# Attention over two problems on one core: a new start, new load costs and a new projection rate

## Chip, cores, metric

One core of a Trainium2 chip. The metric is the device time of one launch in microseconds (us). The four executions of one kernel lie within 0.6 to 7.7 us of each other. The experiments ran on several chips; each is given as a ratio to the kernel before, run beside it on the same chip.

## The reference, cut to what matters

Two problems, A and B, of the same shapes, each a cross-attention against a stored K and V:

```python
# B=16 batches, Sq=144 queries, D=448, H=16 heads, Sk=512 keys, Dh=256, bf16
q = (x @ wq).reshape(B, Sq, H, Dh).transpose(0, 2, 1, 3)
scores = jnp.einsum("bhqd,bhkd->bhqk", q, k_cache) * (Dh ** -0.5)
p = softmax(scores)
o = jnp.einsum("bhqk,bhkd->bhqd", p, v_cache)
out = o.transpose(0, 2, 1, 3).reshape(B, Sq, H * Dh) @ wo
# result: concatenate([A's out, B's out], axis=-1)
```

K and V are 16 x 16 x 512 x 256 values each per problem: 268 MB in all, read once.

## The kernel before

A *unit* is one (problem, batch, head). Units 0 to 255 are A, 256 to 511 are B. For each unit TensorE computes Q (a head of x times wq), S = K Q, P.V, row sums, and some units later a few pieces of the output projection. Exponentials are ScalarE's, most evictions VectorE's.

Every load goes through one queue in program order, issued by SyncE. If the load at its head has to wait for a buffer, all behind it wait too. There are these loads:

- K of the first 48 units in its natural form (2 units a load, 512 KB), transposed by TensorE. They use the same ring of 9 buffers as V.
- From unit 48 on, K by transposing loads of 16 units (4.2 MB), called *K waves* here: wave 0 for unit 48, wave 13 for unit 256 (B's first), wave 15 for unit 288.
- V, 2 units a load, 512 KB. x in groups of batches, wq by heads, wo in 8 parts. B's wq and wo can be loaded only when A's are used up.

The order in the queue is made when the kernel is built, by a planner that gives each load an estimated duration:

```python
def t_load_v(G):
    sl = v_seq["v", G] % NV                  # NV = 9 buffers, shared with natural K
    ...
    S.add(SP, e, writes=[(("v", sl), ("v", G))], dma_sem="v%d" % sl, name="v%d" % G)
...
load(first_q[g0], ..., 1.3 + 0.55 * (g1 - g0), t_load_x, XG)
load(u0 - ls(u0), ..., 2.0 + 0.97 * (u1 - u0), t_load_k, W)
load(first_h[pr, h0], ..., 0.65 * (h1 - h0), t_load_wq, pr, h0, h1)
load(wo_use[pr, wg], ..., 1.3, t_load_wo, pr, wg)
load(UV * G, None, 1.44, t_load_v, G)
```

The projection's pieces are spread over the units by a rate; a piece is done when there is credit:

```python
OP_DELAY, OP_START, OP_RATE = 2, (28, 16), (1.04, 1.15)
...
credit += OP_RATE[i >= NU + OP_START[1]] * NCH * NWO / NU
```

## Time and profile before

| | before |
|---|---|
| time, median of the three executions known then (range) | 1055.7 us (1053.1 to 1056.2) |
| TensorE busy | 1029.9 us, 98% of the span |
| matmuls at their pitch | 1024.3 us |
| lost before the last matmul | 21.8 us |
| of it ahead of unit 16, at unit 288 | 10.9 us, 9.2 us |
| load engines busy | nine tenths or more in every slice but the last two |

The useful quantity is *lost time*: the start of a matmul in the trace, less what all matmuls before it take at their pitch (their usual time from start to start). The 34 constant matmuls and the 24 transposes of x of the new kernel are not counted as work here. Lost time stays flat where TensorE is fed, and each hole is a step in it. The pitches are rounded: with the medians of the trace (0.0625, 0.1225, 0.189 and 0.056 us) the sum is 1020.6 us and the loss 25.5, the difference being spread evenly over the span. So its steps, and differences between kernels at one unit, say more than its absolute value. A wait is given below either as the idle time that a view shows or as the time between two matmul starts over the pitch, which is some 0.2 us more. The two busy rows together say that two resources are busy nearly all the time, TensorE and the loads.

### The profile page before, as it was taken

How to read it: one execution, taken by the hardware profiler on the slowest of the kernel's cores; microseconds unless marked ns; L12 is line 12 of the kernel's file. 1: busy time of each engine (PE TensorE's matmuls, PEld its weight loads, DVE VectorE, ACT ScalarE, POOL GpSimd, SP SyncE). 2: the span in 40 equal slices, each digit the busy share in tenths (PEclk: the TensorE clock that was granted, in tenths of full speed). 3: DMA queues.
4: the chain of work that ended last, by engine and by line, in shares of the span. 5: the costliest groups of instructions: out<-in, count | busy, mean ns of one | idle time of the engine just before them, and what ended most of it. 6: DMA issues, size and time to landing. Idle time of an engine off the chain costs nothing.

```text
span 1051.6 us, 32329 instructions
## 1 busy us (share of the span) xinstructions
PE 1029.9 (98%) x12376; PEld 875.8 (83%) x12376; DVE 737.7 (70%) x2039; ACT 794.1 (76%) x2365; POOL 636.2 (61%) x1030
## 2 busy tenths in 40 slices
PE   7999999999999999999999799999999999999998
PEld 6999888888888888888888688888888888888885
DVE  5776676777776776676777567677776667777775
ACT  5877677777777787777877567787877777788785
POOL 3555556666666666666756456566666666666673
PEclk9999999999999999999999999999999999999999
DMA  9999999999999999999999999999999999999950
GB/s 291 363 341 340 263 306 266 288 288 293 290 300 284 285 237 257 302 290 297 265 288 340 268 276 300 295 272 300 282 269 269 299 258 305 302 271 257 289 187 14
DMA packets 591748, 294.14 MB, mean 280 GB/s; under 512 B 502592, under 2 KB 516768, under 8 KB 591584
## 3 DMA queue, kind: packets, MB, share of 16 engines
q1 hardware_dynamic: 591584, 291.99, 110.1%
q8 instruction: 99, 1.62, 0.6%
q14 instruction: 65, 0.53, 0.2%
HBM read 161.48 MB, written 4.13 MB: 157 GB/s over the span
## 4 chain that ended last, share of the span: by engine, by line
PE 90%; DMA 6%; SPq 1%; ACT 1%; DVE 1%; issue 0%; POOL 0%; ACTq 0%; DVEq 0%
PE s_ps L1112 23%; PE ot_ps L1168 23%; PE qp_ps L1081 22%; PE op_ps L1284 19%; DMA kt_sb<-in_B_k_cache_dram 2%; DMA kt_sb<-in_A_k_cache_dram 2%; PE ot_ps L1184 2%; DMA wq_sb<-in_A_wq_dram 1%; PE qp_ps L1032 1%; PE s_ps L1032 1%; PE qp_ps L1284 1%; ACT rinv_sb L1205 1%; DMA v_sb<-in_B_v_cache_dram 0%; SPq L1002 0%; ACT pt_sb L1122 0%
## 5 line engine op out<-in xcount | busy, mean ns | idle before, releaser
L1132 POOL TENSOR_TENSOR pp_sb<-pt_sb 128x288 f32<-128x288 bf16 x512 | 384.6, 751 | 320.1 <-ACT pt_sb L1122 305.4
L1122 ACT ACTIVATE pt_sb<-s_ps 128x288 bf16<-128x288 f32 x1024 | 364.6, 408 | 182.7 <-PE s_ps L1112 176.5
L1220 DVE TENSOR_TENSOR ring<-ot_ps,rinv_sb 128x288 bf16<-128x288 f32 (+2 forms) x640 | 241.8, 394 | 159.4 <-ACT rinv_sb L1205 155.0
L1112 PE MATMUL s_ps<-qt_sb,kt_sb 128*128 128x144 bf16 x4096 | 341.3, 227 | 8.0 <-DMA kt_sb<-in_B_k_cache_dram 6.9
L1168 PE MATMUL ot_ps<-pt_sb,v_sb 128*128 128x144 bf16 x4096 | 340.2, 226 | 0.3 <-DMA v_sb<-in_A_v_cache_dram 0.2
L1112 PEld LDWEIGHTS s_ps<-qt_sb,kt_sb 128*128 128x128 bf16 x4096 | 288.3, 98 | 60.0 <-issue 7.3
L1205 ACT ACTIVATE rinv_sb<-ln_sb 64x144 f32<-64x144 f32 x928 | 298.3, 321 | 24.2
L1081 PE MATMUL qp_ps<-xt_sb,wq_sb 128*128 128x288 bf16 (+1 forms) x2368 | 302.3, 271 | 2.2 <-DMA wq_sb<-in_A_wq_dram 1.2
L1284 PE MATMUL op_ps<-wo_sb,ring 128*128 128x448 bf16 x1120 | 285.5, 352 | 0.0
L1081 PEld LDWEIGHTS qp_ps<-xt_sb,wq_sb 128*128 128x128 bf16 x2368 | 212.7, 98 | 77.1 <-DVE qt_sb L1094 2.3
L1168 PEld LDWEIGHTS ot_ps<-pt_sb,v_sb 128*128 128x128 bf16 x4096 | 274.3, 98 | 1.2 <-DMA v_sb<-in_A_v_cache_dram 0.4
L1137 POOL TENSOR_TENSOR p_sb<-pp_sb 128x144 f32<-128x144 f32 x464 | 227.4, 490 | 74.2 <-DVE ps_sb L1146 9.4
L1235 DVE TENSOR_REDUCE run_sb<-ot_ps 128x1 bf16<-128x144 f32 x560 | 146.5, 304 | 76.7 <-ACT ln_sb L1192 42.6
L1146 DVE TENSOR_TENSOR ps_sb<-p_sb 64x144 bf16<-64x144 f32 x464 | 156.1, 336 | 45.8 <-POOL p_sb L1137 32.5
L1095 DVE CAST qt_sb<-qp_ps 128x576 bf16<-128x576 f32 x216 | 162.1, 750 | 14.0 <-PE qp_ps L1081 10.9
L1284 PEld LDWEIGHTS op_ps<-wo_sb,ring 128*128 128x128 bf16 x1120 | 93.7, 98 | 20.1
L1192 ACT ACTIVATE ln_sb<-ot_ps 128x144 f32<-128x144 f32 x232 | 67.9, 293 | 32.3 <-PE ot_ps L1184 24.5
L1184 PE MATMUL ot_ps<-ps_sb,ones 128*128 128x144 bf16 x280 | 63.3, 226 | 0.0
L1094 DVE CAST qt_sb<-qp_ps 128x288 bf16<-128x288 f32 x80 | 35.8, 447 | 2.8 <-PE qp_ps L1081 2.6
L1040 ACT ACTIVATE kt_sb<-qp_ps 128x512 bf16<-128x512 bf16 x48 | 28.9, 603 | 6.1 <-PE qp_ps L1032 6.1
L1137 POOL TENSOR_TENSOR ps_sb<-pp_sb 128x144 bf16<-128x144 f32 x48 | 23.5, 490 | 6.9 <-PE ot_ps L1184 0.3
L1184 PEld LDWEIGHTS ot_ps<-ps_sb,ones 128*128 128x128 bf16 x280 | 27.4, 98 | 0.0
(29 smaller groups left out, 154.5 us busy)
## 6 DMA issues: line engine op xcount, KB each, us to landing
v_sb<-in_A_v_cache_dram SPq DMA_DIRECT2D x128, 512.0 KB, 6.9
v_sb<-in_B_v_cache_dram SPq DMA_DIRECT2D x128, 512.0 KB, 7.0
v_sb<-in_A_k_cache_dram SPq DMA_DIRECT2D x22, 512.0 KB, 9.9
out_dram<-ost_sb SPq DMA_DIRECT2D x36, 112.0 KB, 6.1
wo_sb<-in_A_wo_dram SPq DMA_DIRECT2D x8, 448.0 KB, 8.5
wo_sb<-in_B_wo_dram SPq DMA_DIRECT2D x8, 448.0 KB, 8.7
wq_sb<-in_B_wq_dram SPq DMA_DIRECT2D x4, 768.0 KB, 9.3
wq_sb<-in_A_wq_dram SPq DMA_DIRECT2D x3, 768.0 KB, 9.2
```

Of the source, the lines that this page charges most:

```text
L1081: ins = t.matmul(acc, lhsT=wq_sb[:, kc, c0:c0 + 128], rhs=xt_sb[:, kc, xo:xe + 1:max(xe - xo, 1), :], start=(kc == 0), stop=(kc == 3))
L1095: return v.tensor_copy(qt_sb[:, a:b + 1:b - a, :, :], qp_ps[:, :, 0:2 * SQ].rearrange("p e (u q) -> p u e q", u=2))
L1112: ins = t.matmul(s_ps[bank][:, (c % 2) * SQ:(c % 2 + 1) * SQ], lhsT=kt_sb[:, 2 * c + dc, ko:ko + 128], rhs=qt_sb[:, qsl, dc, :], start=(dc ...
L1122: return a.activation(pt_sb[:, psl, 2 * k:2 * k + 2, :].rearrange("p b q -> p (b q)"), s_ps[bank][:, 0:2 * SQ], AF.Exp, scale=DH ** -0.5)
L1132: return g.tensor_tensor(pp_sb[:, :, :], pt_sb[:, psl, 0:2, :], pt_sb[:, psl, 2:4, :], op=ALU.add)
L1137: return g.tensor_tensor(dst, pp_sb[:, 0, :], pp_sb[:, 1, :], op=ALU.add)
L1146: return v.tensor_tensor(ps_sb[p0:p0 + 64, sl, :], p2_sb[0:64, :], p2_sb[64:128, :], op=ALU.add)
L1168: ins = t.matmul(ot_ps[ob][:, dc * SQ:(dc + 1) * SQ], lhsT=v_sb[:, vsl, j, c * DH + dc * 128:c * DH + (dc + 1) * 128], rhs=pt_sb[:, sl, c, ...
L1205: return a.activation(rinv_sb[p0:p0 + 64, sl, :], ln_sb[h0:h0 + 64, :], AF.Exp, scale=-1.0)
L1220: ins = v.tensor_tensor(ring[:, 2 * h:2 * h + 2, r0:r0 + q1 - q0], ot_ps[ob][:, 0:2 * SQ].rearrange("p (c q) -> p c q", c=2)[:, :, q0:q1], ...
L1235: return v.tensor_reduce(run_sb[:, k, j:j + 1], ot_ps[ob][:, 2 * SQ:3 * SQ], axis=AX.X, op=op)
L1284: ins = t.matmul(acc[0:m, 0:D], lhsT=ring[:, c, col0:col0 + m], rhs=wo_sb[:, c, :], start=(c == op_first), stop=(c == op_last))
```

## The change

Five parts. Intent of each: (A) get TensorE to its first P.V sooner: the first two batches of x come by a plain load and are transposed on TensorE, constant matmuls bring the clock up, ScalarE issues the first wq loads. (B) better load costs in the planner, and a rule that puts a load of x right behind a K wave; this also places one more V load ahead of wave 0. (C) fewer projection pieces in units 200 to 240, more in 240 to 292, so that TensorE needs the waves around the problem boundary later. (D) the second Q of a step moves behind P.V. (E) the last eviction is shared by VectorE and ScalarE.

Cut to its core, with three comments added:

```diff
-    OP_DELAY, OP_START, OP_RATE = 2, (28, 16), (1.04, 1.15)
-    MARGIN, HOLD = 1.0, 1.0
+    WARM = 34
+    XR, X_AT = 48, {0: -4, 1: -3}
+    OP_DELAY, OP_START, OP_RATE = 2, (28, 16), ((200, 1.04), (240, 0.7), (292, 1.5), (600, 1.1))
+    MARGIN, HOLD, K_FIX = 1.0, 1.0, 2.4
 ...
+            t_load_wq(0, 0, 1, ACT)
+            t_load_wq(0, 1, 2, ACT)
 ...
+                for _ in range(WARM):
+                    ins = t.matmul(op_ps[:, 0:128], lhsT=ones[:, :], rhs=ones[:, :], start=True, stop=True)
 ...
+        def t_load_xn(g):          # plain load of x, 48 rows to a partition block
+        def t_tr_x(g):             # 12 transposes on TensorE, evicted by VectorE then ScalarE
 ...
-                load(first_q[g0], ..., 1.3 + 0.55 * (g1 - g0), t_load_x, XG)
+                load(first_q[g0], ..., 2.0 + 0.55 * (g1 - g0), t_load_x, XG)
-                load(u0 - ls(u0), ..., 2.0 + 0.97 * (u1 - u0), t_load_k, W)
+                load(u0 - ls(u0), ..., K_FIX + 0.97 * (u1 - u0), t_load_k, W)
-                    load(first_h[pr, h0], ..., 0.65 * (h1 - h0), t_load_wq, pr, h0, h1)
+                    load(first_h[pr, h0], ..., 0.78 * (h1 - h0), t_load_wq, pr, h0, h1)
 ...
-        first = [(t_load_n, (0, 0)), (t_load_x, (0,)), (t_load_wq, (0, 0, 1)), (t_load_n, (0, 1))]
+        first = [(t_load_xn, (0,)), (t_load_n, (0, 0)), (t_load_n, (0, 1)), (t_load_xn, (1,))]
 ...
+                if after_k and m[3] is t_load_x and start <= now:
+                    best = (start, latest, m, lo)
+                    break
 ...
-            now += m[2] - (1.0 if m[3] is t_load_k and dma_plan and dma_plan[-1][0] is t_load_k else 0.0)
+            now += m[2] - (1.4 if after_k and m[3] in (t_load_k, t_load_x) else 0.0)
 ...
-            for u in of_step(lq, i):
+            for u in of_step(lq, i)[:1]:
 ...
+            for v in of_step(lq, i)[1:]:      # behind P.V
+                if q_pair(v):
+                    t_q(v)
+                    t_evac_q(v)
```

More of the change, by code (lines that the diff above doesn't have):

```diff
@@ L798, in bass_concat_heads__mha_block_cached__gqa_block_cached__near_ridge_kernel @@
     assert KR % KW == 0 and NU % KW == 0 and KW % KG == 0
-    X_GROUPS = ((0, 1), (1, 2), (2, 6), (6, 10), (10, 14), (14, 18), (18, 20), (20, 24), (24, 28), (28, 32))
+    X_GROUPS = ((2, 6), (6, 10), (10, 14), (14, 18), (18, 20), (20, 24), (24, 28), (28, 32))
     assert X_GROUPS[-1][1] == NP * Bn and H == KW
-    WQ_GROUPS = ((0, 1), (1, 2), (2, 4), (4, 8), (8, 12), (12, 16))
+    WQ_GROUPS = ((2, 4), (4, 8), (8, 12), (12, 16))
+    WARM = 34
     NQT, NPT, NPS, NRI, NOST = 11, 4, 2, 2, 2
@@ L868, in bass_concat_heads__mha_block_cached__gqa_block_cached__near_ridge_kernel @@
             sem_names.append("n%d" % i)
+        for i in range(NX):
+            sem_names.append("xn%d" % i)
         for i in range(NWG):
@@ L911, in t_init, with e3 @@
             S.add(DVE, e2, writes=[("wqz", 0)], name="wqz")
+            def e3(g):
+                return g.memset(xt_sb[64:128, 3, :, :], 0.0)
+            S.add(DVE, e3, writes=[(("xt", g), g) for g in range(NX)], name="xz")
             def e4(g):
@@ L915, in t_init, with e6 @@
             S.add(POOL, e4, writes=[("ones", 0)], name="ones")
+            def e6(t):
+                ins = None
+                for _ in range(WARM):
+                    ins = t.matmul(op_ps[:, 0:128], lhsT=ones[:, :], rhs=ones[:, :], start=True, stop=True)
+                return ins
+            S.add(PE, e6, reads=[("ones", 0)], writes=[("opp", ("warm", 0))], banks=["op"], name="FAR")
             def e5(g):
@@ L920, in t_init, with t_load_wq @@
             S.add(POOL, e5, reads=[("ones", 0)], writes=[id_key], name="ident")
-        def t_load_wq(pr, h0, h1):
+        def t_load_wq(pr, h0, h1, eng=SP):
             cols = slice(h0 * DH, h1 * DH)
@@ L930, in e @@
                 return q.dma_start(wq_sb[0:64, 3, cols], w[384:448, cols]).then_inc(sems[sem], 16)
-            S.add(SP, e, writes=[(("wq", h), pr) for h in range(h0, h1)], dma_sem=sem, n_dma=2,
+            S.add(eng, e, writes=[(("wq", h), pr) for h in range(h0, h1)], dma_sem=sem, n_dma=2,
                   name="wq%d.%d" % (pr, h0))
@@ L941, in e @@
                     sems["wo%d" % wg], 16)
-            S.add(SP, e, writes=[(("wo", wg), pr)], dma_sem="wo%d" % wg, name="wo%d.%d" % (pr, wg))
+            over = [(("xn", g), 1) for g in range(NX) if pr == 0 and wg in x_rows(g)[2]]
+            S.add(SP, e, writes=[(("wo", wg), pr)] + over, dma_sem="wo%d" % wg, name="wo%d.%d" % (pr, wg))
         def t_load_x(XG):
@@ L977, in t_load_x, with x_rows, e, e1 @@
                   name="x%d" % XG)
+        def x_rows(g):
+            n = SQ // XR
+            c0 = NWO - (NX - g) * n
+            return n, wo_sb[0:XR, c0:c0 + n, :], sorted(set(c // WOG for c in range(c0, c0 + n)))
+        def t_load_xn(g):
+            n, dst, _wgs = x_rows(g)
+            def e(q):
+                return q.dma_start(dst, xs[0][g].rearrange("(t p) d -> p t d", p=XR)).then_inc(sems["xn%d" % g], 16)
+            S.add(SP, e, writes=[(("xn", g), 0)], dma_sem="xn%d" % g, name="xn%d" % g)
+        def t_tr_x(g):
+            n, src, _wgs = x_rows(g)
+            acc = op_ps[:, :].bitcast(BF16)[:, 0:4 * SQ].rearrange("p (c q) -> p c q", c=4)
+            def e(t):
+                ins = None
+                for c in range(4):
+                    m = min(128, D - c * 128)
+                    for k in range(n):
+                        ins = t.transpose(acc[0:m, c, k * XR:(k + 1) * XR], src[:, k, c * 128:c * 128 + m],
+                                          ident[0:XR, 0:XR])
+                return ins
+            S.add(PE, e, reads=[(("xn", g), 0), id_key], writes=[("opp", ("x", g))], banks=["op"], name="TX%d" % g)
+            def e1(v):
+                return v.tensor_copy(xt_sb[:, 0:3, g, :], acc[:, 0:3, :])
+            S.add(DVE, e1, reads=[("opp", ("x", g))], writes=[(("xt", g), g)], banks=["op"], name="exd%d" % g)
+            def e2(a):
+                return a.activation(xt_sb[0:64, 3, g, :], acc[0:64, 3, :], AF.Copy)
+            S.add(ACT, e2, reads=[("opp", ("x", g))], writes=[(("xt", g), g)], banks=["op"], name="exa%d" % g)
         def t_load_k(W):
@@ L1299, in t_evac_op, with e @@
             key = "opp" if bank == "op" else "qp"
-            if eng == ACT:
-                def e(a):
-                    return a.activation(ost_sb[0:m, sl, :], acc[0:m, 0:D], AF.Copy)
-            else:
-                def e(v):
-                    return v.tensor_copy(ost_sb[0:m, sl, :], acc[0:m, 0:D])
-            S.add(eng, e, reads=[(key, ("o", r))], writes=[(("ost", sl), r)], banks=[bank], name="eop%d" % r)
+            parts = ((ACT, 0, D),) if eng == ACT else ((DVE, 0, D // 2), (ACT, D // 2, D))
+            for eng, c0, c1 in parts:
+                def e(g, eng=eng, c0=c0, c1=c1):
+                    if eng == ACT:
+                        return g.activation(ost_sb[0:m, sl, c0:c1], acc[0:m, c0:c1], AF.Copy)
+                    return g.tensor_copy(ost_sb[0:m, sl, c0:c1], acc[0:m, c0:c1])
+                S.add(eng, e, reads=[(key, ("o", r))], writes=[(("ost", sl), r)], banks=[bank], name="eop%d" % r)
         def t_store(r):
@@ L1342, in op_schedule @@
                 fifo["op"].sort(key=lambda t: t[0])
-                credit += OP_RATE[i >= NU + OP_START[1]] * NCH * NWO / NU
+                credit += next(r for u, r in OP_RATE if i < u) * NCH * NWO / NU
                 if i >= NT - H - 14:
@@ L1400, in load_list @@
             for XG, (g0, g1) in enumerate(X_GROUPS):
-                load(first_q[g0], (g1 - NX) * H - lq(NT) if g1 > NX else s_min, 1.3 + 0.55 * (g1 - g0), t_load_x, XG)
+                load(first_q[g0], (g1 - NX) * H - lq(NT) if g1 > NX else s_min, 2.0 + 0.55 * (g1 - g0), t_load_x, XG)
             for W, (u0, u1) in enumerate(WAVES):
                 last = u1 - 1 - KR
-                load(u0 - ls(u0), last - ls(last) + 1 if last >= 0 else s_min, 2.0 + 0.97 * (u1 - u0), t_load_k, W)
+                load(u0 - ls(u0), last - ls(last) + 1 if last >= 0 else s_min, K_FIX + 0.97 * (u1 - u0), t_load_k, W)
             for pr in range(NP):
                 for h0, h1 in WQ_GROUPS if pr == 0 else [(h, h + 4) for h in range(0, H, 4)]:
-                    load(first_h[pr, h0], NU - H + h1 - lq(NU) if pr else s_min, 0.65 * (h1 - h0), t_load_wq, pr, h0, h1)
+                    load(first_h[pr, h0], NU - H + h1 - lq(NU) if pr else s_min, 0.78 * (h1 - h0), t_load_wq, pr, h0, h1)
                 for wg in range(NWG):
                     load(wo_use[pr, wg], wo_done[pr - 1, wg] + 1 if pr else s_min, 1.3, t_load_wo, pr, wg)
+            for g in X_AT:
+                load(X_AT[g], s_min, 0.4, t_load_xn, g)
             for u in range(4):
@@ L1426, in bass_concat_heads__mha_block_cached__gqa_block_cached__near_ridge_kernel @@
             best = None
+            after_k = len(dma_plan) and dma_plan[-1][0] is t_load_k
             for m in todo[:60]:
@@ L1470, in bass_concat_heads__mha_block_cached__gqa_block_cached__near_ridge_kernel @@
                 t_store(stores.pop(0)[0])
+            for g in X_AT:
+                if X_AT[g] == i:
+                    t_tr_x(g)
             u = i + LT
```

## The prediction

> **What bounds the kernel now.** I read the page's first part, then the slices, then the waits, the chain and the timeline around each wait. The first part says that TensorE is busy for nearly the whole span:
>
> ```profile
> PE 1029.9 (98%) x12376; PEld 875.8 (83%) x12376; DVE 737.7 (70%) x2039; ACT 794.1 (76%) x2365; POOL 636.2 (61%) x1030
> ...
> DMA  9999999999999999999999999999999999999950
> ```
>
> Matmul busy time is no proof of a full engine, so I laid the matmul starts in the trace beside the program order. Start to start they are 0.063 us for a 144-column matmul, 0.123 for 288 columns, 0.190 for the output projection and 0.056 for a K transpose. All 12,376 of them at these pitches come to 1024.3 us. The last one starts at 1046.1 us, so 21.8 us are lost before it, and 5.5 us follow it (last eviction and store). Where the 21.8 us lie: 9.2 before unit 0's first P.V matmul, 10.9 by unit 16, 12.1 by unit 48, 12.5 by unit 272, 21.7 by unit 288, and then no more. So there are two holes, the start and one place near 600 us. In the waits view (engine, line waited for: us, times, longest):
>
> ```profile
> PE s_ps L1112 <- DMA kt_sb<-in_B_k_cache_dram: 6.9, 1, 6.9
> ...
> PE s_ps L1032 <- DMA v_sb<-in_A_k_cache_dram: 6.1, 2, 3.9
> ...
> PEld qp_ps L1081 <- DVE qt_sb L1094: 2.3, 7, 1.1
> ...
> PE qp_ps L1081 <- DMA wq_sb<-in_A_wq_dram: 1.2, 2, 0.9
> ...
> PE s_ps L1112 <- DMA kt_sb<-in_A_k_cache_dram: 0.3, 1, 0.3
> ```
>
> The first line is the hole at 600 us; the lines of v_sb and wq_sb are the start; the longest wait for qt_sb, 1.1 us, is one place, at 112 us, where two Q projections in one step wait for one bank. The chain of waits names the two K waves (a wave is the transposing load of K for 16 units) that arrived just too late: start, time to landing.
>
> ```profile
> 96.78 20.41 DMA kt_sb<-in_A_k_cache_dram
> ...
> 576.58 25.29 DMA kt_sb<-in_B_k_cache_dram
> ```
>
> And the timeline shows what the start and the hole look like:
>
> ```profile
> 1.27 1.32 SPq L964 DMA_TRANSPOSE xt_sb<-in_A_x_dram  x1
> ...
> 3.92 0.60 PE L1032 MATMUL s_ps<-qt_sb,v_sb 128*128 128x128 bf16 x4 [3.92 <-DMA v_sb<-in_A_k_cache_dram]
> ...
> 4.50 1.21 SPq L964 DMA_TRANSPOSE xt_sb<-in_A_x_dram  x1
> ...
> 7.49 1.17 PE L1081 MATMUL qp_ps<-xt_sb,wq_sb 128*128 128x144 bf16 x8
> ...
> 13.79 0.66 PE L1081 MATMUL qp_ps<-xt_sb,wq_sb 128*128 128x144 bf16 x8
> ...
> 602.01 1.12 PE L1112 MATMUL s_ps<-qt_sb,kt_sb 128*128 128x144 bf16 x8 [6.88 <-DMA kt_sb<-in_B_k_cache_dram]
> ...
> 603.88 2.12 PE L1081 MATMUL qp_ps<-xt_sb,wq_sb 128*128 128x288 bf16 x8
> ...
> 608.35 0.66 PE L1112 MATMUL s_ps<-qt_sb,kt_sb 128*128 128x144 bf16 x8
> ```
>
> Eight equal matmuls take 1.17 us at 7.49 and 0.66 at 13.79, and after the 6.9 us wait 1.12 us until about 606.5: the array runs at half speed after idling. So the hole costs 7.0 us of wait and 2.2 us of slow matmuls, 9.2 us.
>
> **What the Trainium skill says.** "TensorE: Matmul & The Clock Gate", section "What's actually happening": the array runs at half clock until it has been busy for a window of about 3.4 us, and falls back after an idle one. The trace agrees: 5 us of slow matmuls from 7.1 to 12.4 us, 4.5 us from 602.0. "DMA: Bandwidth & Descriptors", section "Issuing engines are not separate DMA queues": issuing from ScalarE saves only the issuing engine's time. The trace has what can be saved: two x transposes held SyncE 1.32 and 1.21 us, each wq issue 0.57 us. "PSUM — Partial Sum Buffer", section "Terms": two engines on the same bank and partitions at once collide, reads included. So a split eviction has to be serial, and the new program does make ScalarE's half wait for VectorE's.
>
> **The change part by part.** The matmul counts are the same but for 34 constant matmuls and 24 small x transposes, and every matmul that follows has the same pitch.
>
> *Start.* The constants begin at about 1.1 us (their operand is written by 1.0 us) and fill the array to 1.1 + 34 x 0.107 = 4.7 us (0.107 us is the start-to-start time of 128-column matmuls before 12 us), so it is at full speed by about 6. But the first Q is not earlier: x's 12 transposes (about 1 us) start at 4.7, their eviction is VectorE then ScalarE (some 0.45 + 0.3 us plus hand-overs), and the second x's transposes, which stand ahead of the first Q on TensorE, wait for that: the first Q at about 7.5, as now. From there, steps run at full speed (Q 0.5, S 0.5, evictions 0.45 between) instead of half: P.V of unit 0 at about 12.7 against 15.0. The loads also run ahead: the first V lands at 14.4 us now, although 2.8 MB at 0.385 MB/us from 3 us on would be there at 10.3; I take 3.5 us for that lead. The stalls of units 0 to 16 (1.7 us now) are all on loads and should mostly go. Lead at unit 16: about 3.5 us.
>
> *First K wave.* The new order puts one more V load (1.35 us, landing to landing) ahead of it. That load waits for the P.V of unit 37 and is therefore early only as TensorE is. Wave: 117.2 + 1.2 - 3.5 = 114.9 us, or by the backlog of loads 114.6. Needed: 116.8, less 1.07 for the second Q moved behind P.V, less 3.5, is 112.2. So TensorE waits some 2.6 us at unit 48, and of the lead only 117.3 - 114.8 = 2.5 us remain.
>
> *Problem boundary.* Eight wo loads, four wq pairs and 17 V loads lie between two waves here. Landing to landing, now: wave at 517.5, next 559.5, next 601.9, that is 42.0 and 42.3 us. The rate change moves projection pieces in program order: at unit 240 the new kernel has done 28 fewer (x 0.19 = 5.3 us earlier), at unit 272 the same number, at unit 288 some 12 more (2.3 us later). Chain in the new order: wave for unit 240 at 481.1 (now 486.8; gate 5.7 us earlier, its x load moved behind it), unit 256 at 481.1 + 28.5 = 509.6, unit 272 at 509.6 + 42.0 + 2 V (2.7) = 554.3 against a need of 560.6, unit 288 at 554.3 + 42.3 + one store (0.4) = 597.0. Need: 594.9 now without the wait, + 2.3 - 2.5 = 594.7. A wait of 2.3 us remains in place of 7.0, too short, I think, for the half clock. Unit 304's wave: 597.0 + 25.8 + V, store and x load (4.2) = 627.0, need about 629. After that the slack grows. Saved here: 9.2 - 2.3 = 6.9 us.
>
> *End.* The last eviction is one 0.62 us instruction; halved and serial it is two of about 0.35 us and a hand-over: 0.15 us more.
>
> Sum: 2.5 + 6.9 - 0.15 = 9.2 us. From 1055.7 that is 1046.5; as the three runs scatter over 3 us and the profiled one took 1053.4, I say 1046.
>
> **Rivals.** (a) Both waits vanish: the full lead of 3.5, the 1.07 and 0.5 us at unit 48, and 9.2 us: 14 us, 1042 us. For it: all later waves have 6 to 12 us of slack now, and the rates look chosen to fit. Against: the landing sums above. (b) Loads become the bound at the boundary: the faster stretch 200 to 240 needs 16 units in 30 us, and a wave (17.3 us from the landing before it to its own) plus 8 V (10.8), a store and a share of x also take about 30 us. If each load is 1 us worse than I took it, the wait at unit 288 returns to 5 or 6 us with the half clock, and unit 304 waits too: gain 2 to 4 us, 1052. Against: the wave for unit 272 has 6 us of slack even then. (c) The start gives nothing, because the first wave takes all of it back: then only the boundary counts, 1048.5. (d) ScalarE, which now issues four wq loads (about 2.2 us) ahead of its first eviction, delays the opening; it is idle until 4.99 us now, so at most a few tenths.
>
> **Range and chances.** The floor is 1024.3 of matmuls, about 7 at the start with the x transposes, and 5.5 at the end: 1037, plus 2 to 3 between span and time, 1040. Two per cent faster would be 1034.6, under that floor, so it is nearly excluded; slower by 2% would need new waits of 30 us. Range 1040.5 to 1051.5.
>
> **What would show it.** Right: the first Q at 7 to 8 us but its eight matmuls in 0.66; a TensorE wait of 2 to 3 us for the A wave near 112 us; the B wave wait at unit 288 down to 0 to 4 us and no slow matmuls behind it; lost time over pitch about 12.5 us. Wrong: no wait near 112 us (the start's lead was then kept), another wait at unit 272 or 304, or slow matmuls around 600 us.

## The result, and the profile after

| | before | after |
|---|---|---|
| time, median of 4 runs each (range) | 1054.8 (1053.1 to 1056.2) | 1057.3 (1056.4 to 1058.7) |
| ratio, 95% interval | | 1.0026 (1.0005 to 1.0046) |
| span of the profiled run | 1051.6 | 1055.4 |
| lost time at unit 511 | 21.9 | 25.4 |

A ratio is the mean time of one kernel's fast runs over that of the other's fast runs of the same rounds, so it is not quite the ratio of the two medians. Nothing was gained; if anything the kernel is a quarter of a per cent slower. The prediction was 1046.0.

Two lines of the page of the kernel after: busy time of the engines, and the chain of waits by engine.

```profile
PE 1033.3 (98%) x12434; PEld 877.9 (83%) x12434; DVE 738.3 (70%) x2042; ACT 794.4 (75%) x2368; POOL 635.9 (60%) x1030
...
PE 86%; DMA 11%; ACT 1%; SPq 1%; DVE 1%; issue 0%; POOL 0%; ACTq 0%; DVEq 0%
```

TensorE is as full as before, and 11% of the chain is now loads (6% before). Its waits (engine, line, what for: us, times, longest):

```profile
PE ot_ps L1220 <- DMA v_sb<-in_B_v_cache_dram: 5.0, 2, 3.8
PE s_ps L1164 <- DMA kt_sb<-in_A_k_cache_dram: 3.7, 1, 3.7
PE s_ps L1164 <- DMA kt_sb<-in_B_k_cache_dram: 3.2, 3, 2.3
PE op_ps L1018 <- DMA wo_sb<-in_A_x_dram: 2.0, 1, 2.0
```

The wait for B's K fell from 6.9 us to 2.3. Four other waits took its place: for V of B, for A's first K wave, for two more waves of B, and for the plain load of x (it lands in the space of wo). The chain shows when these loads were issued and how long they took (start, us to landing):

```profile
2.21 5.75 DMA wo_sb<-in_A_x_dram
...
95.92 22.49 DMA kt_sb<-in_A_k_cache_dram
...
578.35 25.02 DMA kt_sb<-in_B_k_cache_dram
...
608.87 27.28 DMA kt_sb<-in_B_k_cache_dram
```

And the timeline of TensorE at the places where time was lost (start, us, what; in brackets the idle time just before):

```profile
4.80 0.74 PE L1018 MATMUL op_ps<-qt_sb,wo_sb 48*128 48x48 bf16 x12
...
8.09 0.58 PE L1018 MATMUL op_ps<-qt_sb,wo_sb 48*128 48x48 bf16 x12 [2.00 <-DMA wo_sb<-in_A_x_dram]
...
8.98 1.17 PE L1133 MATMUL qp_ps<-xt_sb,wq_sb 128*128 128x144 bf16 x8
...
15.54 0.66 PE L1220 MATMUL ot_ps<-pt_sb,v_sb 128*128 128x144 bf16 x8
...
118.55 1.12 PE L1164 MATMUL s_ps<-qt_sb,kt_sb 128*128 128x144 bf16 x8 [3.66 <-DMA kt_sb<-in_A_k_cache_dram]
119.46 1.17 PE L1220 MATMUL ot_ps<-pt_sb,v_sb 128*128 128x144 bf16 x8
...
603.50 0.66 PE L1164 MATMUL s_ps<-qt_sb,kt_sb 128*128 128x144 bf16 x8 [2.30 <-DMA kt_sb<-in_B_k_cache_dram]
...
761.51 0.66 PE L1220 MATMUL ot_ps<-pt_sb,v_sb 128*128 128x144 bf16 x8 [3.82 <-DMA v_sb<-in_B_v_cache_dram]
```

The constants did bring the clock up: the transposition of x at 4.80 is followed by fast ones. But the second one waits 2.0 us for its load, and the first Q behind it takes 1.17 us for eight matmuls, half speed again. The first P.V stands at 15.5 us, against 15.0 before. At 118.55 the first K wave is 3.7 us late and the clock is slow for two groups behind it. At 603.5 the wait is short and the clock stays up. At 761.5 there is a wait that the kernel before does not have.

Lost time in us by the start of a unit, in profiled runs (the last two columns belong to experiments told below):

| unit | before | after | after, again | wave 0 moved |
|---|---|---|---|---|
| 40 | 10.6 | 9.1 | 10.5 | 7.6 |
| 64 | 12.0 | 14.4 | 15.9 | 8.3 |
| 200 | 11.8 | 14.2 | 15.7 | 8.1 |
| 280 | 12.5 | 15.9 | 17.3 | 9.7 |
| 288 | 21.7 | 18.3 | 21.4 | 12.0 |
| 511 | 21.9 | 25.4 | 22.2 | 15.6 |

So by unit 64 the change has lost 2.4 us where it should have gained 2.5; at unit 288 it saves most of the big hole as foreseen; and behind it, where the kernel before loses nothing, this run lost 7 us more. In the repeat (third column) it lost 0.8 us there, so that part is chance, as told below.

### The profile page after: what moved, and what is told of

Read it like the earlier page. It is cut to its first block, busy times and chain, and to the rows that moved or that the text cites. A ratio compares the mean times of both kernels' runs of the same rounds, so it can differ in the third digit from the quotient of the medians.

```text
span 1055.4 us, 32451 instructions
## 1 busy us (share of the span) xinstructions
PE 1033.3 (98%) x12434; PEld 877.9 (83%) x12434; DVE 738.3 (70%) x2042; ACT 794.4 (75%) x2368; POOL 635.9 (60%) x1030
## 4 chain that ended last, share of the span: by engine, by line
PE 86%; DMA 11%; ACT 1%; SPq 1%; DVE 1%; issue 0%; POOL 0%; ACTq 0%; DVEq 0%
PE s_ps L1164 22%; PE ot_ps L1220 22%; PE qp_ps L1133 21%; PE op_ps L1336 17%; DMA kt_sb<-in_B_k_cache_dram 8%; DMA kt_sb<-in_A_k_cache_dram 2%; PE ot_ps L1236 1%; PE s_ps L1084 1%; PE qp_ps L1084 1%; DMA v_sb<-in_B_v_cache_dram 1%; PE qp_ps L1336 1%; DMA wo_sb<-in_A_x_dram 1%; ACT rinv_sb L1257 0%; SPq L1054 0%; DVE ring L1272 0%
## 5 line engine op out<-in xcount | busy, mean ns | idle before, releaser
L1336 PEld LDWEIGHTS op_ps<-wo_sb,ring 128*128 128x128 bf16 x1120 | 94.0, 98 | 21.4
```

The source lines that it names most:

```text
L1336: ins = t.matmul(acc[0:m, 0:D], lhsT=ring[:, c, col0:col0 + m], rhs=wo_sb[:, c, :], start=(c == op_first), stop=(c == op_last))
```

## The experiments

### First: which part does what

Four kernels on one chip, three rounds, beside the kernel before (1054.3 us there). *e1_old_rate* is the kernel after without part C:

```diff
-OP_RATE = ((200, 1.04), (240, 0.7), (292, 1.5), (600, 1.1))
+OP_RATE = ((272, 1.04), (600, 1.15))
```

> The changed kernel with the projection rate of before (1.04, from unit 272 on 1.15). Theory 1 (a debt of the load queue: the loads of the problem boundary cannot be carried in the time there is, and moving projection work only moves the wait): the wait at unit 288 comes back to 6 to 8 us, the later waits for V and K (0.9, 1.0, 4.0, 1.3 us) shrink by as much, the time stays within 2 us of the changed kernel. Theory 2 (order: the new load costs put V behind K and x): the rate was worth its 7 us, so the time rises by 4 us or more, to about 1061, with the later V waits still there.

Measured: 1058.1 us, ratio 1.0041 (1.0011 to 1.0072). The wait at unit 288 is back and larger than before, 9.3 us between matmuls, and behind it nothing over 0.4 us is left.

*e2_rate_only* is the kernel before with part C alone:

```diff
-OP_RATE = (1.04, 1.15)
+OP_RATE = ((200, 1.04), (240, 0.7), (292, 1.5), (600, 1.1))
```

> The kernel before with nothing changed but the projection rate. Theory 1: the wait of 7.0 us at unit 288 falls to 2 to 3 and comes back at later units in pieces, time within 2 us of before. Theory 2: with the old load costs nothing comes back, the time falls by 5 us or more, to about 1049.

Measured: 1053.7 us, ratio 0.9981 (0.9959 to 1.0002). There is no wait at unit 288 at all, but others stand elsewhere, the largest being this one near 552 us:

```profile
PE qp_ps L1081 <- DMA wq_sb<-in_B_wq_dram: 3.5, 1, 3.5
```

*e3_old_costs* is the kernel after without part B (costs and rule of before):

```diff
-K_FIX 2.4; x 2.0 + 0.55n; wq 0.78n; chained 1.4; rule "x right behind a K wave"
+K_FIX 2.0; x 1.3 + 0.55n; wq 0.65n; chained 1.0 (K only); no rule
```

> The changed kernel with the load costs of before in its planner (K wave, x, wq) and without the rule that puts an x load right behind a K wave. One V load fewer stands ahead of the first K wave, so the wait at unit 48 (3.8 us) should fall by about 1.3 us. Theory 1: the waits behind unit 288 stay in sum (about 7 us) at other places, time 1 to 2 us below the changed kernel. Theory 2: the V waits vanish, time 6 us or more below, about 1050.

Measured: 1055.6 us, ratio 1.0002 (0.9984 to 1.0020). The first wave is 2.0 us late instead of 3.8, with 24 V loads ahead of it instead of 25, and the wait for wq of B is 5.6 us.

*e4_start_only* is the kernel after with the edits of e1 and e3 together, so new start, moved Q and shared last eviction alone:

> The kernel before with the new start, the moved second Q and the split last eviction, but old rates and old load costs. If the first K wave is what takes the start's lead back, its landing hardly moves (117 us) and the time equals before within 1.5 us, with a wait of 2 to 3 us at unit 48. If instead the extra V load was to blame, the lead is kept and the time is 2 us below before.

Measured: 1055.5 us, ratio 0.9998 (0.9966 to 1.0030). TensorE has lost 9.3 us at unit 40, 1.3 less than before, and 13.2 at unit 64, 1.2 more. What the start gives, the first K wave takes back with interest.

From these four: each part moves the waits to another place, and the sums hardly differ. Two theories fit. Either there is simply too much to load, so that any wait saved is a debt to be paid later; or some load has a bad place in the queue.

### Second: are the waits at the boundary a matter of bytes?

*f1_after_no_wo* and *f2_before_no_wo* cut the eight loads of B's wo to 16 of 448 columns, in the kernel after and the one before. Their outputs are wrong, which doesn't matter for the times. The order of all instructions is unchanged.

```diff
-return q.dma_start(wo_sb[:, c0:c0 + WOG, :], w[...])
+n = D if pr == 0 else 16
+return q.dma_start(wo_sb[:, c0:c0 + WOG, 0:n], w[..., 0:n])
```

> The kernel after, with each load of the second problem's projection weights cut to 16 of its 448 columns; the order of all instructions is unchanged and the result is wrong on purpose. About 8 loads of 1.2 us shrink to a fraction, so some 7 to 9 us less have to be moved shortly ahead of unit 288. Theory (the loads set the pace, a wait that is saved at the boundary is a debt that is paid later): the 2.5 us wait at unit 288 and the later waits of 0.9, 1.0, 4.0 and 1.3 us go or shrink to under 2.5 us in sum; lost time over the matmul pitch by unit 511 about 17 instead of 25.4, time 1048 to 1051 (0.6 to 0.9% less than after). Rival (the later waits come from the order of loads there, whatever happened before): the 4.0 us wait for V at about 757 us stays, only the 2.5 us at unit 288 goes, time 1054 to 1055.

> The kernel before with the same cut (wrong on purpose). Theory (the wait at unit 288 is the place where a shortage of load time shows, not a fault of the projection rate): the 7.1 us wait and the 2.2 us of slow clock behind it go almost wholly; lost time by unit 511 about 13 instead of 21.8, time 1045 to 1047. Rival (the wait is set by buffers that TensorE frees late, not by bytes): wait still over 5 us, time over 1051.

Measured: f1 1048.8 us, ratio 0.9945 (0.9921 to 0.9969); f2 1046.8 us, ratio 0.9927 (0.9908 to 0.9946). In f1 no wait of TensorE is left between 560 and 870 us, lost time is 16.2 us at unit 288 and 16.0 at the end. In f2 it is 12.6 at unit 288, and the waits in that stretch are down to this:

```profile
PE ot_ps L1170 <- DVE ps_sb L1148: 0.9, 1, 0.9
```

So the hole at unit 288 is a wait for bytes, in both kernels. Both expectations were met. For the waits behind unit 288, f1 shows less than it seems to: g1 and h1 below, whose loads at the boundary are uncut, have none there in their traces either (20.0 us lost at unit 288 and 19.4 at the end; 20.7 and 20.3). Wave 15 landed 3.1 us before it was needed in f1, and 0.6 us in f2.

### Third: the start and the first K wave

*f3_x1_early* is the kernel after with the second plain load of x ahead of the first two loads of K:

```diff
-first = [xn0, n0.0, n0.1, xn1]
+first = [xn0, xn1, n0.0, n0.1]
```

> The kernel after with the second plain load of x ahead of the two first loads of K instead of behind them. First step (the second transposition of x waited only for its late load): its 2.2 us gap near 6 us goes or falls under 1 us, and the slow clock of 8.6 to 11.9 us with it; lost time by unit 16 falls from 9.6 by 1 to 3 us. Second step, theory (the first K wave is set by loads): the wait for it grows by the same and the lost time by unit 64 stays 14 to 15.5, whole time within 0.15% of after. Rival (the lead is kept): lost time by unit 64 about 12, time 1055 or less.

Measured: 1056.5 us, ratio 1.0021 (0.9999 to 1.0042). The first step failed: the wait for x went, but a wait of 1.3 us for K took its place, the clock was slow again at 9.6 us, and lost time at unit 16 is 9.1 us against 9.5. The start stayed short of loads in this order too. The second step held: the wait for the first wave grew to 4.8 us (in f1, with the order of after, it was 5.2, so this alone proves little).

*g1_wave0_relieved* cuts three of A's eight wo loads, which stand ahead of wave 0 (GpSimd writes zeros into the rest once). Its output is wrong, which doesn't matter for the time.

```diff
+S.add(POOL, memset wo_sb[:, 0:12, 16:448])
+n = 16 if pr == 0 and wg < 3 else D
```

> The kernel after with three of the eight loads of the first problem's projection weights cut to 16 of 448 columns (wrong on purpose; GpSimd fills the rest with zeros once at the start). Some 3 us less are moved ahead of the first K wave. Theory (the first K wave is late because of what is moved ahead of it): its wait of 3.8 us falls to 1 us or none, and the slow clock behind it goes too; lost time by unit 64 falls from 14.5 to 10.5 to 11.5. Whole time: 2 to 4 us less than after if the gain is kept, as later waits are for loads too, and these were all brought forward by 3 us. Rival (wave 0 waits for its buffer or its issue): wait still over 3 us.

Measured: 1056.6 us, ratio 1.0024 (1.0000 to 1.0048), and the wait is hardly smaller:

```profile
PE s_ps L1172 <- DMA kt_sb<-in_A_k_cache_dram: 3.1, 1, 3.1
```

The theory that bytes alone decide fell here. The last natural K load ahead of the wave landed at 90.9 us instead of 94.9, yet the wave was issued at 96.2 against 95.9. With fewer bytes ahead, something else holds it up. SyncE's own lines in the kernel after say what (start, us, what; a group includes its waits):

```profile
85.56 1.14 SPq L1069 DMA_DIRECT2D v_sb<-in_A_k_cache_dram  x1
89.83 6.04 SPq L1054 DMA_DIRECT2D v_sb<-in_A_v_cache_dram  x4
95.92 19.78 SPq L1040 DMA_TRANSPOSE kt_sb<-in_A_k_cache_dram  x1
115.75 1.09 SPq L1054 DMA_DIRECT2D v_sb<-in_A_v_cache_dram  x2
```

and its waits between 86 and 97 us:

```profile
SPq L1054 <- PE qp_ps L1084: 7.4, 2, 4.3
```

Two V loads were issued at 90 us. The next waits 4.3 us for TensorE's K transposes (line 1084) of unit 41, which hold its buffer. The wave, whose own buffer is free all the time, stands behind it in the in-order queue.

Two things keep this from being the whole cause. First, the hold is not new. In the kernel before, the same V load waits in the same way, and the wave is issued even later than in the kernel after, at 96.78 against 95.92:

```profile
91.22 5.52 SPq L1002 DMA_DIRECT2D v_sb<-in_A_v_cache_dram  x3
96.78 17.70 SPq L988 DMA_TRANSPOSE kt_sb<-in_A_k_cache_dram  x1
```

Second, an earlier issue alone does not help either. In f1, whose edit lies far behind this point, TensorE was by chance 1.4 us further ahead at unit 40 than in the first trace of after, and the wave went out 1.4 us earlier. It still landed at 118.5 us:

```profile
88.41 6.04 SPq L1056 DMA_DIRECT2D v_sb<-in_A_v_cache_dram  x4
94.50 22.01 SPq L1042 DMA_TRANSPOSE kt_sb<-in_A_k_cache_dram  x1
```

Take away bytes, and buffers hold the wave; bring the buffers forward, and the loads ahead of it do. What all 20 traces share is that the wave lands 16.4 to 19.2 us after the load just ahead of it in the queue.

### Fourth: move the wave, nothing else

*h1_after_k0_early* is the kernel after with wave 0 three V loads earlier, ahead of the V load of units 44 and 45:

```diff
+k0, v0 = dma_plan.index((t_load_k, (0,))), dma_plan.index((t_load_v, (22,)))
+dma_plan.insert(v0, dma_plan.pop(k0))
+due.insert(v0, due.pop(k0))
```

> The kernel after with one load moved: the first K wave is issued ahead of the V load of units 44 and 45 instead of three V loads later, where it stood behind a V load whose buffer came free only with P.V of unit 37. Theory (the first K wave is late because of its place in the in-order queue behind a V load that waits for a buffer, not because of bytes): issue at about 90.3 us instead of 95.9, landing at 112 to 114.5 instead of 118.4, the 3.8 us wait and the slow clock behind it gone or under 0.5 us, lost time by unit 64 9.0 to 10.5 instead of 14.4. The V loads now behind it land by 118, needed from 117.4: a wait of up to 1 us there is possible. Whole time: if what is saved is kept, 1052 to 1054; if it comes back as waits behind unit 288 (loads set the pace from there), 1055 to 1058 as after. Rival (landing follows the bytes moved before): landing over 117.

Measured: 1051.0 us, ratio 0.9963 (0.9946 to 0.9980). The wave was issued at 91.7 and landed at 114.2, 6.1 us before its use. But the V load that it overtook is now late:

```profile
PE ot_ps L1220 <- DMA v_sb<-in_A_v_cache_dram: 2.4, 1, 2.4
```

So the place in the queue decides when the wave lands, but three steps are one too many. Lost time at unit 64 is 15.1 us, where 9.0 to 10.5 were expected; the start of this run had been slow by 1.4 us more than in the first run of after. By unit 64 this trace has thus gained nothing on the kernel after. It is shorter because it loses nothing behind unit 288, so its time does not show what the move is worth.

*h2_e3_k0_early* and *h3_before_k0_early* make the same move in e3 and in the kernel before.

> The same move on the kernel after with the load costs of before. Expect the wait for the first K wave (2.0 us without the move) gone, lost time by unit 64 9 to 10.5 instead of 11.65; the 5.6 us wait for wq of the second problem near 552 us stays or grows by up to 2 us, as its load is released by TensorE's progress and by the loads ahead of it. Time 1053 to 1056.

> The same move on the kernel before. Its wait for the first K wave was only 0.5 us and its wait at unit 288 7.1 us. Expect the 0.5 us gone, lost time by unit 64 11.4 to 12, and at unit 288 a wait of 6 to 8 us as before if that wait is set by the loads between units 224 and 288 (theory), or 2 to 4 us if the 5 us that the first K wave lands earlier are handed on by all loads (rival). Time 1053 to 1055 by the theory, 1050 to 1052 by the rival.

Measured: h2 1058.1 us, ratio 1.0032 (1.0015 to 1.0049); h3 1058.9 us, ratio 1.0043 (1.0027 to 1.0060). Both times missed what was expected, for the same reason: a V wait (2.2 and 3.1 us) where the first wave had cost 2.0 and 0.5. The wait at unit 288 of h3 stayed at 7.1 us, as the theory had it. h3 teaches one thing more. It has lost 4.3 us more than before by unit 64, and 4.9 us more at the end: what is lost at the first wave is not absorbed by anything later.

*e5_no_x_rule* is the kernel after without the rule for x:

```diff
-if after_k and m[3] is t_load_x and start <= now:
-    best = (start, latest, m, lo)
-    break
```

> The kernel after without the rule that puts a load of x right behind a K wave. If that rule made the 4.0 us wait for V near 757 us: it falls under 2 us and the time to 1054 to 1055. If the wait is the debt of loads: as much waiting behind unit 288 in sum (6 to 8 us), at other places, and 1056 to 1058.

Measured: 1054.5 us, ratio 1.0000 (0.9983 to 1.0017). The 4 us wait for V is gone, but the wait at unit 288 is 3.6 us, with slow clock behind it, 6.4 us together. Neither expectation fits whole; on its own this run does not say what the rule is worth for the time.

### Fifth: the right place, and the kernel after once more

Four kernels on one chip (before: 1054.6). *i5_after_again* is the kernel after, unchanged.

> The kernel after, unchanged, beside the others on one chip. If its order of loads makes the waits behind unit 288: 1056 to 1058.5 and 4 to 8 us of waits for K and V behind unit 300. If the chip of the first run made them: 1051 to 1054 and under 2 us of such waits.

Measured: 1055.7 us (1053.4 to 1058.3), ratio 1.0015 (0.9990 to 1.0040). The profiled execution took 1054.1. It waits 3.6 us for the first wave and 2.4 us at unit 288, and behind that only for this:

```profile
PE ot_ps L1220 <- DMA v_sb<-in_B_v_cache_dram: 0.9, 1, 0.9
```

So the 7 us behind unit 288 belong to one execution, not to the order alone. (The waits fit the second expectation, the median time of 1055.7 neither.) At unit 288 this execution came out of its wait with slow clock (timeline of TensorE):

```profile
604.93 1.03 PE L1164 MATMUL s_ps<-qt_sb,kt_sb 128*128 128x144 bf16 x8 [2.27 <-DMA kt_sb<-in_B_k_cache_dram]
605.75 1.17 PE L1220 MATMUL ot_ps<-pt_sb,v_sb 128*128 128x144 bf16 x8
```

It had lost 21.4 us there instead of 18.3, of which 1.6 are slow clock; so TensorE reached the next wave 1.6 us after it landed, where in the first trace it reached it too early.

*i1_k0_ahead_v23* moves wave 0 two V loads up instead of three:

```diff
-dma_plan.index((t_load_v, (22,)))
+dma_plan.index((t_load_v, (23,)))
```

> The kernel after with the first K wave two V loads earlier than there, ahead of the V load of units 46 and 47. Theory (place in the queue): issue at about 91 us, landing at 114.5 to 116, no wait of TensorE over 0.7 us between 105 and 125 us, lost time by unit 64 9 to 10.5; if the start loses more by chance, as in other runs, then by what unit 40 shows more. Whole time 1046 to 1050. Rival: wait for K or V of over 1.5 us there, 1050 to 1053.

Measured: 1049.6 us (1047.6 to 1050.9), ratio 0.9956 (0.9939 to 0.9973). SyncE's lines and TensorE's:

```profile
88.33 0.88 SPq L1054 DMA_DIRECT2D v_sb<-in_A_v_cache_dram  x2
89.25 19.41 SPq L1040 DMA_TRANSPOSE kt_sb<-in_A_k_cache_dram  x1
108.71 2.86 SPq L1054 DMA_DIRECT2D v_sb<-in_A_v_cache_dram  x4
```

```profile
7.31 0.58 PE L1018 MATMUL op_ps<-qt_sb,wo_sb 48*128 48x48 bf16 x12 [0.91 <-DMA wo_sb<-in_A_x_dram]
...
8.06 0.66 PE L1133 MATMUL qp_ps<-xt_sb,wq_sb 128*128 128x144 bf16 x8
...
13.48 0.66 PE L1220 MATMUL ot_ps<-pt_sb,v_sb 128*128 128x144 bf16 x8
...
113.63 0.73 PE L1164 MATMUL s_ps<-qt_sb,kt_sb 128*128 128x144 bf16 x8 [0.25 <-ACT pt_sb L1174]
```

The wave is issued straight behind the two V loads whose buffers are free, lands at 112.3, and unit 48 waits for nothing but an exponential. It beats the kernel before by 5.0 us of median, and the kernel after, beside it on the same chip, by 6.1. By luck this profiled execution also shows nearly the start that had been predicted: the second x is only 0.9 us late, the first Q runs at full speed, and the first P.V stands at 13.5 us.

What the move gives apart from that luck is read from unit 40 to unit 64: 0.7 us are lost there in i1, against 5.3 and 5.4 in the two traces of after, and 0.9 to 2.4 in the four further runs below that make the same move. It does two things at once. It takes the wave out from behind the load that waits for a buffer, and it puts two V loads behind the wave, which took 3.1 us to land ahead of it in the first trace of after. No run separates the two.

*i2_k0_v23_no_x_rule* leaves out the rule for x as well (edit of e5), and *i3_k0_v23_no_x_rule_x1* also takes the early x (edit of f3).

> As the run before it, without the rule that puts x right behind a K wave. Start the same; the wait at unit 288 3.5 to 5 us instead of 2.5 (x and one more V load stand ahead of wave 15), and behind it under 1.5 us of waits in sum. Time 1046 to 1050, within 0.2% of the run before it if loads set the pace.

> As the run before it, with the second plain load of x ahead of the first two loads of K. The gap of TensorE ahead of the second transposition of x falls by 0.5 to 1.5 us; with no wait at the first K wave to take it back, lost time by unit 64 falls by as much. Time 0 to 1.5 us under the run before it.

Measured: i2 1050.3 us, ratio 0.9958 (0.9942 to 0.9975); i3 1050.2 us, ratio 0.9963 (0.9935 to 0.9991). Both are i1 within the scatter, so the rule for x and the order at the start decide nothing of the time. In i2 the wait at unit 288 is 3.9 us and one of 0.7 follows, as expected; but V was 1.7 us late near 140 us, which was not. What the rule for x does is plain in the landings. Without it (e5, i2, i3) wave 16 lands 26.1 to 26.4 us after wave 15 and TensorE comes to it 7.1 to 8.8 us later; with it (after, its repeat, g1, h1, i1, f3) it lands 32.1 to 32.8 us after wave 15, and at most 1.7 us of slack are left. In exchange the wait at unit 288 is shorter (2.4 to 2.5 us against 3.6 to 4.2). The time is the same within the scatter.

### Sixth: is the rate worth something once the wave is in time?

*i4_k0_v23_old_rate* is i1 with the rates of before (edit of e1). *j1_k0_v23_start24* is i1 with B's projection starting at unit 280 instead of 272:

```diff
-OP_START = (28, 16)
+OP_START = (28, 24)
```

> The kernel after with the first K wave ahead of the V load of units 46 and 47 and with the projection rates of before. If a wait saved at unit 288 is paid later (debt): wait at 288 of 7 to 9.5 us, under 1.5 us of waits behind it, time within 0.2% of the kernel with the new rates (1048 to 1051.5). If the new rates are worth their part of the prediction: 1053 to 1056.

> The kernel after with the first K wave ahead of the V load of units 46 and 47, and the second problem's projection starting at unit 280 instead of 272. Its eight weight loads move four V loads back but stay ahead of the wave of unit 288, with two more V loads: the wait there stays or grows to 2 to 6 us, time 1049 to 1053. Under 1048 would be a surprise that speaks for a relief there.

Measured: i4 1056.3 us, ratio 1.0011 (0.9992 to 1.0029); j1 1055.8 us, ratio 1.0014 (0.9998 to 1.0031). The theory of debt fell with i4: with the old rates the gain of the moved wave is gone, and nearly all of it at one place.

```profile
607.75 1.12 PE L1164 MATMUL s_ps<-qt_sb,kt_sb 128*128 128x144 bf16 x8 [11.10 <-DMA kt_sb<-in_B_k_cache_dram]
```

Part of this is the planner: with the old rates it puts two more V loads ahead of wave 15 (146 instead of 144), so i4 tells the worth of the rate together with the order that the planner makes of it. j1 has 146 too, and waits 8.5 us at unit 288. That is worse than the 2 to 6 us expected; the later start relieved nothing.

## Why the prediction was wrong

Two steps failed. The first is the lead: the start was to gain 3.5 us, and 2.5 of them were to survive the first K wave, which was to land at 114.9 us. It landed at 118.4, and by unit 64 the kernel was 2.4 us behind the kernel before. The second is "after that the slack grows": there was hardly any, and the first trace lost 7.1 us there.

Predicted lost time was 12.5 us; the first trace has 25.4. The difference of 12.9 us splits as follows. (The pitches that the prediction prints are rounded and come to 1027.0 us, not to its 1024.3; that shifts every lost time alike along the span and touches none of these steps.)

**Start: lead of 3.5 us at unit 16.** Measured 1.4 us, and in other executions of the same start 0 to 2.9. The step "P.V of unit 0 at about 12.7" failed: it was 15.5. I had the second x transposition wait for its bank only; it waited 2.0 us for its load, which took 5.75 us from issue. With that idle time the clock fell back, and two Q groups ran at 1.17 us. The Trainium skill, "TensorE: Matmul & The Clock Gate", section "What's actually happening", calls the window free-running and the warm-up variable from run to run. The traces agree that the outcome varies: 0.9 us of idle time left the Q behind it at 0.66 us, 2.0 us made it 1.17. The same page, section "Part 4: PE-mode transpose", says that transposes do not count as busy in the same way; that would explain why 2 us sufficed here, as only transposes surround the wait. No run separates it, and it is not needed: at unit 288 of the repeat a wait of 2.3 us among ordinary matmuls was followed by slow ones too. That the rest of the mechanism was right, i1's profile shows, where the second x came only 0.9 us late by luck, with the first P.V at 13.5.

**First K wave: a wait of 2.6 us, 2.5 us of lead left.** The wait was 3.8 us with slow clock behind it, so at unit 64 the kernel had lost 14.4 us, 2.4 more than before, where 2.5 less were predicted: 5.0 us with what the start lacked. The sum that failed is "117.2 + 1.2 - 3.5 = 114.9": the wave landed 3.5 us later. The V load of units 46 and 47, the last ahead of the wave before, landed only 1.55 us earlier, as the lead was 1.4 and not 3.5 (2.0 us of the miss). The added V load took 1.6 us and not 1.2 (0.4). The wave landed 17.8 us after the load ahead of it, where it had taken 16.7 before (1.1). The slow clock behind the wait, which was not foreseen, makes some 1.3 us more. That the gate moves with TensorE was right: this V load was issued at 94.98 us, before at 96.37. More lead would not have carried through, though: in f1, 2.8 us ahead at unit 40, the wave still landed at 118.5.

What the prediction did not ask is whether the wave has to stand there at all. In both kernels it stands behind V loads that wait for a buffer (4.3 us in the kernel after), while its own is free. Taking it two places forward is worth 6.1 us of median beside the same kernel (i1), 0.6%; with the hold it also gets rid of the transfer of two V loads, and how much is due to each is not shown.

**The stretch to the boundary.** TensorE's loss from unit 200 to 280 grew by 1.6 us instead of 0.7 before. I had counted with 5.3 us less projection there, which the traces show: units 224 to 240 took 28.8 us instead of 31.1. But the loads did not come faster: from wave 11's landing to wave 13's it is 60.3 us, against 59.6 before, where I had used 28.5 for the last step alone. "Wave for unit 240 at 481.1" failed: it came at 490.0. It was to be let go 5.7 us earlier than before, when TensorE is done with unit 223; it was issued at 467.05, before at 467.01, and then took 22.9 us to land instead of 19.8.

**Boundary: 2.3 us of wait instead of 7.0, no slow clock.** The wait came out right: 2.47 us between matmuls, lost time 2.4 us, and full speed behind it. But its terms did not. The landing of wave 15 was put at 597.0 and came at 603.4, and TensorE needed it 6.3 us later, too; the two errors cancel. The 5.0 us lost by unit 64 and the 0.9 of the stretch explain most of both. The full speed was luck: six traces with this order of loads have a wait of 2.35 to 2.47 us here; in i5 (the repeat), f3, g1 and h1 slow clock followed and cost another 1.6 us, in after and i1 it did not.

**"After that the slack grows."** Wrong. Wave 16 was to land 30.0 us after wave 15; it took 32.8 us in the first trace and 32.1 in the repeat, and TensorE needs 31.9 us for these 16 units (from 603.50 to 636.29 in the first trace, less 0.88 of waiting). So there is hardly any slack for the next waves. The rule for x, with the order that the planner then makes, takes it: without the rule wave 16 lands 26.1 to 26.4 us after wave 15. Under the rule, whether 1 or 7 us are lost is decided by chance: by the slow clock at unit 288 (the two traces without it, after and i1, lost 7.1 and 3.6 us behind it, the four with it at most 1.4), and by how quickly the V loads and stores between the waves pass, which took some 5 us longer between waves 15 and 22 of the first trace than in h1, in the same order. What makes them slower in one execution stays open.

**End.** Two serial halves of 0.39 and 0.36 us, predicted 0.35 each.

The sum: 5.0 (start and wave 0) + 0.9 (stretch) + 0.1 (boundary) + 7.1 (behind it) = 13.1, against 12.9; 0.2 of the 7.1 were lost before, too. In the repeat the same four terms are 6.4, 0.9, 1.8 and 0.8. So the first term and the stretch stand in both traces, and the other two change places by chance.

Of the rivals, (c), that the first wave takes the start back, is what e4 and f3 showed. (b) was right that unit 304 would wait too, but it took the loads themselves to be slower; that the whole wave could go ahead of the loads which hold it, no part of the prediction asked.

One reading of the experiments has to be kept apart. Loads at the boundary are short of bandwidth (f1, f2), but it does not follow that gains ahead of it are lost. In the kernels that share one order of loads behind unit 64, the landing of wave 15 less the time lost by unit 200 is 589.1 us (after), 589.1 (after again), 589.1 (h1), 589.0 (g1) and 589.0 (i1). In the first problem the V loads are released by TensorE's progress, so a microsecond won before unit 200 arrives as a microsecond at unit 288. That is why what one moved load wins near 115 us is still there at the end, and why the 4.3 us lost in h3 are lost for good.

And the rate? It was worth 0.2% in the kernel before (e2), not clearly more than that in the kernel after (e1 against after: 1.0041 against 1.0026 and 1.0015 on other chips), and 0.55%, some 5.8 us, in i1 (1.0011 against 0.9956, on another chip and with the planner's part). Its predicted 6.9 us come nearly in full only where the rest is in time.

## What to carry to other kernels

In an in-order queue, read for each late load not only what it waits for but what the loads ahead of it wait for: a transfer whose buffer is free may belong ahead of one whose buffer is not, and then its bytes go first as well. Move it only so far that the loads which it overtakes still land in time, since here three places made them late (h1, h2, h3) and two did not. Where loads and TensorE are both full, judge a part of a change in the kernel in which the other parts work; alone it only moves the waits.

## What the Trainium skill lacked or had wrong

- "DMA: Bandwidth & Descriptors", section "Issuing engines are not separate DMA queues", calls the sequencer's time to initiate a transfer usually small relative to the transfer. For the transposing loads of K it is most of it: the issue of wave 0 held SyncE for 19.8 us of the 22.5 us to landing, and 19.4 us in i1. The next V load was issued at 115.75 us, right behind it.
- The same page, section "Latency and other measured facts", gives 261 GB/s for a transposing DMA with a non-contiguous dimension. Here, between waves 15 and 22 in the traces of after and h1, 4.19 MB took 16.2 to 18.8 us from the landing before to their own, 223 to 259 GB/s, against 512 KB of V in about 1.35 us (388 GB/s). Whether these loads are of the page's form was not looked into; the spread of one kernel's waves is as large as some of the waits in dispute.
- "TensorE: Matmul & The Clock Gate", section "What's actually happening", has the array fall back after an idle window of about 3.4 us. Idle times of 2.0 us (among transposes) and of 2.27 us (unit 288 in the repeat) were followed by slow matmuls, and one of 2.30 us at the same place in the first trace was not. The page's free-running window may account for the chance, but the page gives no estimate for waits shorter than the window.
- No page draws the consequence that a load which waits for its buffer holds back every later load of its queue, also one that could go: SyncE waited 4.3 us here with a 4.2 MB load behind.
